# Fused linear attention and top-8 MLP on one Trainium2 core: the fifth spread copy moved ahead of a q unit, one product of M put into other PSUM banks, and M's copies put ahead of the q phis

## The chip, the cores and the metric

The kernel runs on one core of one Trainium2 chip. The metric is the device time of one execution in microseconds (us), as the median of the runs shown. Work is spread over the core's engines, each with its own queue of instructions in program order: TensorE (PE; its weight loads are listed apart as PEld), VectorE (DVE), ScalarE (ACT), GpSimd (POOL) and SyncE (SP, which here only issues transfers). They wait for each other through semaphores.

## The reference

The input x has 2048 tokens of width 640. The result is x plus two branches.

```
xn = layernorm(x)
q, k, v = split(xn @ wqkv)                    # 32 heads of 20
phi(t) = where(t > 0, t + 1, exp(t)) + 1e-6
kv = phi(k)^T v ; z = sum over tokens of phi(k)          # per head
o = (phi(q) kv) / (phi(q) z + 1e-6) @ wo

r = x @ w_r ; idx = the 8 tokens with the largest r
y = ((silu(x[idx] @ w_gate) * (x[idx] @ w_up)) @ w_down) * sigmoid(r[idx])
out = x + o + (x with y added at the rows idx)
```

## The kernel before

**Tiles and names.** Tokens stand in 16 tiles of 128, the width 640 in five blocks of 128. `ps` is the whole of PSUM: 8 banks of 512 f32 per partition, given out by number. `xnT` is the normalised input, transposed; `pqT` is phi(q), transposed (five blocks `m` by 2048 tokens). A "q unit" `u` is one block by 512 tokens: five matmuls into one bank (`q_mm`, L244), two ACT operations (`q_act`, L256 and L257: exp and relu) and one DVE operation that joins them into `pqT` (`q_phi`, L263). Units 0 to 12 are made in the main loop; this case is about units 13 to 19.

**Attention as one matrix.** The sum over tokens is made once (`GT`), turned into masked `kvT`, and joined with `wo` into a matrix M of five blocks (`M_sb`, in the tile named `late`). Block `m` of M is four matmuls into two banks (`m_mm`, L627) and one DVE copy out of them (`m_copy`, L636). The output of a token tile is then `pqT` times M (`o_mm`, L757), ten matmuls of 320 columns, plus the residual row (`o_add`, L767), and a store (L774).

**The denominators.** For each half of the tokens (`h`, 1024 tokens), `den_mm` and `den_act` make the inverse denominators `rd`. For each block, `spread_mm` (L570) spreads them over 128 rows: four matmuls into one half of the four banks 0 to 3. A "spread copy" on ACT (L587) moves these 1024 columns into one of the two halves of `spw`, and a DVE multiplication (L591) scales the block of `pqT` with them. Half 0 needs five such copies and scalings before the first output tile; half 1 is done within the output phase (L788 and L794).

**The MLP.** For the 8 chosen tokens, `hm` and its transpose `hT` are made, then come the down products (L712, 48 small matmuls into bank 4), their scaling on DVE into `y_sb` (L719), and an indirect DMA from POOL that adds the eight rows into a DRAM copy of x plus xn (`xxd`, L722). After it SP reloads the residual rows from `xxd` (L729), in pieces of 1, 1, 2, 2 and 2 tiles, then two pieces of four.

**Order.** The kernel is written out by hand (`manual_schedule`): on each engine the instructions stand in the order of the Python text, and the waits between engines follow from which instruction reads or overwrites what. Between the down products and the outputs the text goes on with M's blocks 1 to 4 in banks 6 and 7, q units 14 to 16 in banks 5, 4 and 5, and the fifth spread of half 0; then units 17 to 19 in banks 0, 1 and 2.

Of the kernel before, what the change touches and what calls it, by code (L numbers as in the profile page):

```python
# [9 lines left out]
S = 2048  # L10
# [10 lines left out]
HALF = S // 2  # L21
# [13 lines left out]
ALU = mybir.AluOpType  # L35
# [8 lines left out]
def kernel(  # L44
# [13 lines left out]
    nc = tc.nc  # L58
# [14 lines left out]
    def sb(shape, dt, name, pool=None, tag=None):  # L73
        return (pool or big).tile(shape, dt, tag=tag or name, name=name)
# [4 lines left out]
    pqT = sb([P, KC, S], BF16, "pqT")  # L79
# [29 lines left out]
    ps = psum.tile([P, 8, 512], F32, tag="ps", name="ps")  # L109
# [131 lines left out]
    def q_mm(u, b, lo=0, hi=KC):  # L241
        m, tb = QU[u]
        for kc in range(lo, hi):
            nc.tensor.matmul(  # L244
                ps[:, b, :],
                lhsT=wq_sb[:, kc, m * P : (m + 1) * P],
                rhs=xnT[:, kc, tb * TBLK : (tb + 1) * TBLK],
                start=(kc == 0), stop=(kc == KC - 1),
            )
# [3 lines left out]
    def q_act(u, b):  # L253
        e = evq.tile([P, TBLK], BF16, tag="eq", name=f"eq{u}")
        r = evq.tile([P, TBLK], BF16, tag="rq", name=f"rq{u}")
        nc.scalar.activation(e[:], ps[:, b, :], AF.Exp)  # L256
        nc.scalar.activation(r[:], ps[:, b, :], AF.Relu)  # L257
        qbuf[u] = (e, r)

    def q_phi(u):  # L260
        m, tb = QU[u]
        e, r = qbuf.pop(u)
        nc.vector.scalar_tensor_tensor(  # L263
            out=pqT[:, m, tb * TBLK : (tb + 1) * TBLK], in0=e[:], scalar=1.0, in1=r[:],
            op0=ALU.min, op1=ALU.add,
        )
# [11 lines left out]
    def grest_mm(t, c0, c1, b):  # L278
        for c in range(c0, c1):
            nc.tensor.matmul(  # L280
                ps[:, b, (c - c0) * P : (c - c0 + 1) * P],
                lhsT=xn[:, t, c * P : (c + 1) * P],
                rhs=pk[:, t, 512:D],
                start=(t == 0 and c == c0), stop=(t == T - 1),
                skip_group_check=True,
            )
# [198 lines left out]
    for t in range(T - 1):  # L485
# [3 lines left out]
        out=candm[:], in0=cand[:].unsqueeze(2).to_broadcast([T, 2, T, C]),  # L489
        in1=diag[:].unsqueeze(1).unsqueeze(3).to_broadcast([T, 2, T, C]), op=ALU.mult,  # L490
# [16 lines left out]
    for t in range(9):  # L507
# [11 lines left out]
        out=allc[:], in0=ps[:, 5, P : 2 * P], in1=tileoff[:].rearrange("p t c -> p (t c)"),  # L519
        op=ALU.add,  # L520
# [4 lines left out]
        out=junk[:, 0:C], in0=posu[:], scalar=1.0, in1=oh8[:], op0=ALU.mult, op1=ALU.mult,  # L525
# [3 lines left out]
        out=junk[:], in0=iot[:], scalar=pcol[:, 0:1], in1=allc[:], op0=ALU.is_equal,  # L529
# [4 lines left out]
        out=idxw[:, 1:2], in0=pcol[:, 1:2], scalar1=yoff[:, 0:1], scalar2=yoff[:, 1:2],  # L534
        op0=ALU.mult, op1=ALU.add,
    )
    for i in range(C):
# [5 lines left out]
        out=zm[:], in0=zT[:].rearrange("p (k h) -> p k h", k=KC), in1=headg[:], op=ALU.mult  # L543
# [24 lines left out]
    def spread_mm(h, m, half_bank):  # L568
        for j in range(4):
            nc.tensor.matmul(  # L570
                ps[:, j, 256 * half_bank : 256 * half_bank + 256],
                lhsT=grep[32 * j : 32 * j + 32, m * P : (m + 1) * P],
                rhs=rdens[h][32 * j : 32 * j + 32, :],
                start=True, stop=True, skip_group_check=True,
                tile_position=(32 * j, 0),
            )

    spw = big.tile([P, 2, 4, 256], BF16, tag="wk_sb", name="spw")
    nsp = [0]

    def spread_mul(h, m, half_bank, via_act, then=None, args=()):
        src = ps[:, 0:4, 256 * half_bank : 256 * half_bank + 256]
        dst = pqT[:, m, h * HALF : (h + 1) * HALF].rearrange("p (j f) -> p j f", j=4)
        if via_act:
            w = spw[:, nsp[0] % 2, :, :]
            nsp[0] += 1
            nc.scalar.copy(w, src)  # L587
            src = w
        if then is not None:
            then(*args)  # L590
        nc.vector.tensor_tensor(out=dst, in0=dst, in1=src, op=ALU.mult)  # L591

    den_mm(0, 6)
    den_act(0, 6)
# [29 lines left out]
    def m_mm(m, b):  # L624
        for h in range(2):
            for j in range(2):
                nc.tensor.matmul(  # L627
                    ps[DB * j : DB * j + DB, b + h, 0:HW],
                    lhsT=kvT[:, 2 * m + j, :],
                    rhs=wo_sb[:, 2 * m + j, h * HW : (h + 1) * HW],  # L630
                    start=True, stop=True,
                    tile_position=(0, DB * j),
                )

    def m_copy(m, b):
        nc.vector.tensor_copy(  # L636
            M_sb[:, m, :].rearrange("p (b f) -> p b f", b=2), ps[:, b : b + 2, 0:HW]
        )


    def gu_mm(w, b):
        for kc in range(KC):
            for j in range(4):
                nc.tensor.matmul(
                    ps[32 * j : 32 * j + 32, b, 0:FJ],
                    lhsT=xsT[:, kc, :],
                    rhs=w[:, kc, j * FJ : (j + 1) * FJ],
                    start=(kc == 0), stop=(kc == KC - 1),
                    tile_position=(0, 32 * j),
                )  # L650
# [10 lines left out]
    def q_unit(u, b):  # L661
        q_mm(u, b)
        q_act(u, b)

    nc.vector.scalar_tensor_tensor(
        out=junk[:, 0:C], in0=gv[:], scalar=1.0, in1=oh8[:], op0=ALU.mult, op1=ALU.mult,
# [10 lines left out]
    spread_mm(0, 1, 1)  # L677
    for t in range(9, T):
        grest_mm(t, 0, 4, 7)
    spread_mul(0, 0, 0, True)  # L680
    nc.vector.tensor_copy(
        GT[:, 0:4, 512:D], ps[:, 7, :].rearrange("p (c f) -> p c f", c=4)
    )
    for t in range(T):
        grest_mm(t, 4, 5, 6)
    nc.vector.tensor_copy(GT[:, 4, 512:D], ps[:, 6, 0:P])
    spread_mul(0, 1, 1, True)
    gu_mm(wg_sb, 5)
    nc.scalar.activation(e1, ps[:, 5, 0:FJ], AF.Exp, scale=-1.0)
    kv_mm(8, 10, 6, 8)  # L690
# [12 lines left out]
    q_mm(13, 5, 3)  # L703
    nc.vector.tensor_copy(hT, psb(4)[:, 0:FJ].rearrange("p (b c) -> p b c", b=3))
    m_copy(0, 6)
    spread_mul(0, 2, 0, True)
    spread_mul(0, 3, 1, True)
    q_act(13, 5)
    for fc in range(FC):
        j, b = fc // 3, fc % 3  # L710
# [9 lines left out]
        out=y_sb[:], in0=ps[:, 4, 0:YW], scalar1=gcol[:, 3:4], scalar2=None, op0=ALU.mult  # L720
# [2 lines left out]
        xxd[:], bass.IndirectOffsetOnAxis(ap=idxw[:, 1:2], axis=0), y_sb[:], None,  # L723
        compute_op=ALU.add,
    )
    q_phi(13)

    def reload(t0, t1):
        nc.sync.dma_start(x_sb[:, t0:t1, :], xxd_v[:, t0:t1, :])  # L729
# [2 lines left out]
        reload(t0, t1)  # L732
    m_mm(1, 6)
    m_copy(1, 6)
    spread_mm(0, 4, 0)
    q_unit(14, 5)
    spread_mul(0, 4, 0, True)
    m_mm(2, 6)
    m_copy(2, 6)
    q_phi(14)  # L740
    q_unit(15, 4)
    m_mm(3, 6)
# [2 lines left out]
    q_unit(16, 5)  # L745
    m_mm(4, 6)
    m_copy(4, 6)
    q_phi(16)
    for u in range(17, 20):
        q_unit(u, u - 17)  # L750
# [29 lines left out]
    scaled = []  # L780

    def spread_1(*ms):
        for i, m in enumerate(ms):
            spread_mm(1, m, i)
        for i, m in enumerate(ms):
            w = spw[:, nsp[0] % 2, :, :]
            nsp[0] += 1
            nc.scalar.copy(w, ps[:, 0:4, 256 * i : 256 * i + 256])  # L788
            scaled.append((m, w))

    def scale_1():
        m, w = scaled.pop(0)
        dst = pqT[:, m, HALF:S].rearrange("p (j f) -> p j f", j=4)
        nc.vector.tensor_tensor(out=dst, in0=dst, in1=w, op=ALU.mult)  # L794

    MID = {1: den_1, 2: lambda: spread_1(0, 1), 4: lambda: spread_1(2, 3)}
    END = {2: lambda: reload(8, 12), 4: lambda: reload(12, 16), 5: lambda: spread_1(4)}
    for t in range(T):
        b = (4, 6)[t % 2] if t < 8 else (0, 2, 4, 6)[t % 4]
        if t < T - 1:  # L800
            cols, banks = ((0, HW), (HW, D)), (b, b + 1)
            o_mm(t, cols, banks, 0, 2)
            if t in MID:
                MID[t]()
            o_mm(t, cols, banks, 2)
            o_add(t, b, 0, D)
            o_store(nc.sync if t % 2 == 0 else nc.scalar, t, 0, D)
        else:
            for i, (c0, c1, bb) in enumerate(((0, HW, b), (HW, 512, b + 1), (512, D, 0))):
                o_mm(t, ((c0, c1),), (bb,))  # L810
                o_add(t, bb, c0, c1)
                o_store(nc.scalar if i == 1 else nc.sync, t, c0, c1)
        if t in END:
            END[t]()
        if 2 <= t <= 5:
            scale_1()
        if t == 5:
            scale_1()
# [30 lines left out]
```

## Time and profile before

| What | us |
|---|---|
| median of 3 runs | 117.46 (117.32 to 117.6) |
| the profiled execution | 117.55 |
| its span, first to last instruction | 115.8 |
| PE busy in the span | 107.8 |
| DVE busy | 87.1 |
| ACT busy | 62.1 |
| POOL busy | 33.0 |

The profile is of one execution. It says for each engine how long it was busy, what each idle stretch waited for, and which chain of work ended last. In a row of the timeline the first number is the start in us from the beginning of the span, the second the time; `x4` says that four instructions are merged; in square brackets stands the idle time of the engine just before, and what ended it. `L627` is a line of the kernel.

### The profile page before, as it was taken

How to read it: one execution, taken by the hardware profiler on the slowest of the kernel's cores; microseconds unless marked ns; L12 is line 12 of the kernel's file. 1: busy time of each engine (PE TensorE's matmuls, PEld its weight loads, DVE VectorE, ACT ScalarE, POOL GpSimd, SP SyncE). 2: the span in 40 equal slices, each digit the busy share in tenths (PEclk: the TensorE clock that was granted, in tenths of full speed). 3: DMA queues.
4: the chain of work that ended last, by engine and by line, in shares of the span. 5: the costliest groups of instructions: out<-in, count | busy, mean ns of one | idle time of the engine just before them, and what ended most of it. 6: DMA issues, size and time to landing. Idle time of an engine off the chain costs nothing.

```text
span 115.8 us, 2502 instructions
## 1 busy us (share of the span) xinstructions
PE 107.8 (93%) x922; PEld 62.7 (54%) x922; DVE 87.1 (75%) x182; ACT 62.1 (54%) x123; POOL 33.0 (28%) x85
## 2 busy tenths in 40 slices
PE   5999996999999999999999999997699999999990
PEld 2445453555555555555555688543235666677770
DVE  0867999599997999877898927488695568695571
ACT  1568734755578555687555936593739465500000
POOL 7305357838777664500000023004100000000000
PEclk9999999999999999999999999999999999999999
DMA  3999379806999999999565994000286026985333
GB/s 108 307 378 332 64 175 180 216 0 140 273 229 235 265 369 146 312 365 339 184 226 182 262 382 147 6 0 0 14 230 228 24 89 156 301 282 178 113 113 113
DMA packets 23814, 22.20 MB, mean 192 GB/s; under 512 B 10074, under 2 KB 22522, under 8 KB 23802
## 3 DMA queue, kind: packets, MB, share of 16 engines
q1 hardware_dynamic: 21824, 19.99, 61.2%
q10 hardware_dynamic: 1834, 2.02, 5.1%
q0 software_dynamic: 144, 0.04, 0.5%
q8 instruction: 7, 0.11, 0.4%
q14 instruction: 5, 0.04, 0.1%
HBM read 14.62 MB, written 5.28 MB: 172 GB/s over the span
## 4 chain that ended last, share of the span: by engine, by line
PE 66%; DVE 13%; issue 6%; ACT 5%; DMA 4%; POOLq 3%; POOL 1%; ACTq 0%; DVEq 0%
PE ps L244 17%; PE ps L210 14%; PE ps L757 14%; PE ps L271 11%; DMA xnT<-xn 4%; PE ps L291 3%; POOLq L538 3%; DVE st L165 1%; DVE xn L767 1%; DVE xn L180 1%; DVE pk L233 1%; PE ps L627 1%; ACT spw L788 1%; DVE st L162 1%; PE ps L192 1%
## 5 line engine op out<-in xcount | busy, mean ns | idle before, releaser
L210 PE MATMUL ps<-wk_sb,xnT 128*128 128x320 bf16 (+1 forms) x160 | 25.2, 301 | 1.2 <-DMA xnT<-xn 1.0
L244 PE MATMUL ps<-xnT,wq_sb 128*128 128x512 bf16 x100 | 24.7, 379 | 0.1
L757 PE MATMUL ps<-late,pqT 128*128 128x320 bf16 (+2 forms) x165 | 22.6, 295 | 0.0
L226 ACT ACTIVATE ek<-ps 128x640 bf16<-128x640 f32 x16 | 11.3, 704 | 18.9 <-PE ps L210 18.9
L210 PEld LDWEIGHTS <-xnT 128*128 128x128 bf16 x160 | 15.3, 98 | 10.7 <-DMA xnT<-xn 1.7
L271 PE MATMUL ps<-pk,xn 128*128 128x512 bf16 x80 | 20.1, 379 | 0.2 <-DVE pk L233 0.2
L757 PEld LDWEIGHTS <-pqT 128*128 128x128 bf16 x165 | 15.6, 98 | 6.6 <-issue 0.6
L767 DVE TENSOR_TENSOR xn<-ps,x_sb 128x640 bf16<-128x640 f32 (+3 forms) x18 | 13.1, 748 | 5.6 <-PE ps L757 5.6
L263 DVE SCALAR_TENSOR_TENSOR pqT<-eq,rq 128x512 bf16<-128x512 bf16 x20 | 14.3, 714 | 3.8 <-ACT rq L257 3.8
L233 DVE SCALAR_TENSOR_TENSOR pk<-ek,rk 128x640 bf16<-128x640 bf16 x16 | 13.4, 838 | 3.5 <-ACT rk L227 3.3
L256 ACT ACTIVATE eq<-ps 128x512 bf16<-128x512 f32 x20 | 12.3, 617 | 4.4 <-PE ps L244 4.4
L244 PEld LDWEIGHTS <-wq_sb 128*128 128x128 bf16 x100 | 9.3, 97 | 9.7 <-issue 1.0
L271 PEld LDWEIGHTS <-xn 128*128 128x128 bf16 x80 | 7.7, 98 | 9.4 <-issue 0.5
L257 ACT ACTIVATE rq<-ps 128x512 bf16<-128x512 f32 x20 | 12.3, 616 | 0.0
L171 POOL TENSOR_TENSOR rs<-rs,half 128x1 f32<-128x1 f32 x14 | 11.1, 794 | 1.1
L227 ACT ACTIVATE rk<-ps 128x640 bf16<-128x640 f32 x16 | 11.2, 697 | 0.0
L162 DVE BATCH_NORM_STATS2 st<-x_sb 128x6 f32<-128x320 bf16 x16 | 7.7, 484 | 3.3 <-DMA x_sb<-in_A_x_dram 3.2
L168 POOL TENSOR_TENSOR rs<-mv,half 128x1 f32<-128x1 f32 x14 | 5.3, 377 | 15.6 <-DVE mv L166 15.4
L180 DVE TENSOR_SCALAR xn<-x_sb,mv,rs 128x640 bf16<-128x640 bf16 x16 | 7.7, 484 | 0.9 <-ACT rs L176 0.7
L539 POOL COPY xsT<-xnT 128x5 bf16 x8 | 1.7, 207 | 22.3 <-DMA xxd<-x_sb 18.9
L165 DVE BATCH_NORM_STATS2 st<-x_sb 128x6 f32<-128x320 bf16 x16 | 7.6, 476 | 0.0
L186 DVE TENSOR_TENSOR x_sb<-x_sb,xn 128x640 bf16<-128x640 bf16 x16 | 6.9, 475 | 0.0
(118 smaller groups left out, 103.1 us busy)
## 6 DMA issues: line engine op xcount, KB each, us to landing
x_sb<-in_A_x_dram SPq DMA_DIRECT2D x6, 320.0 KB, 4.3
wg_sb<-in_B_w_gate_dram SPq DMA_DIRECT2D x5, 384.0 KB, 5.2
wu_sb<-in_B_w_up_dram SPq DMA_DIRECT2D x5, 384.0 KB, 4.1
wd_sb<-in_B_w_down_dram SPq DMA_DIRECT2D x3, 640.0 KB, 8.5
xxd<-x_sb SPq DMA_DIRECT2D x2, 640.0 KB, 3.2
out_dram<-xn SPq DMA_DIRECT2D x8, 160.0 KB, 1.9
x_sb<-xxd SPq DMA_DIRECT2D x2, 640.0 KB, 5.4
out_dram<-xn ACTq DMA_DIRECT2D x7, 160.0 KB, 1.8
```

Source lines behind the costliest of these rows:

```text
L171: nc.gpsimd.tensor_tensor(out=rs[:, 1:2], in0=rs[:, 0:1], in1=half[:, 1:2], op=ALU.pow)
L210: nc.tensor.matmul(ps[:, b + h, 0:w], lhsT=xnT[:, kc, t * P : (t + 1) * P], rhs=wk_sb[:, kc, h * HW : h * HW + w], start=(kc == 0), stop=( ...
L226: nc.scalar.activation(e[:], ps[:, b : b + 2, 0:HW], AF.Exp)
L227: nc.scalar.activation(r[:], ps[:, b : b + 2, 0:HW], AF.Relu)
L233: nc.vector.scalar_tensor_tensor(out=pk[:, t, :].rearrange("p (b f) -> p b f", b=2), in0=e[:], scalar=1.0, in1=r[:], op0=ALU.min, op1=ALU.add,
L244: nc.tensor.matmul(ps[:, b, :], lhsT=wq_sb[:, kc, m * P : (m + 1) * P], rhs=xnT[:, kc, tb * TBLK : (tb + 1) * TBLK], start=(kc == 0), stop ...
L256: nc.scalar.activation(e[:], ps[:, b, :], AF.Exp)
L257: nc.scalar.activation(r[:], ps[:, b, :], AF.Relu)
L263: nc.vector.scalar_tensor_tensor(out=pqT[:, m, tb * TBLK : (tb + 1) * TBLK], in0=e[:], scalar=1.0, in1=r[:], op0=ALU.min, op1=ALU.add,)
L271: nc.tensor.matmul(ps[:, c, :], lhsT=xn[:, t, c * P : (c + 1) * P], rhs=pk[:, t, 0:512], start=(t == 0), stop=(t == T - 1),)
L757: nc.tensor.matmul(ps[:, b, 0 : c1 - c0], lhsT=pqT[:, kc, t * P : (t + 1) * P], rhs=M_sb[:, kc, c0:c1], start=(kc == 0), stop=(kc == KC - 1),)
L767: nc.vector.tensor_tensor(out=xn[:, t, c0:c1].rearrange("p (b f) -> p b f", f=w), in0=ps[:, b : b + n, 0:w], in1=x_sb[:, t, c0:c1].rearran ...
```

## The change

Three things change in the part between the down products and the outputs. The fifth spread copy of half 0 stands on ACT ahead of unit 14's two operations, no longer behind them. Block 2 of M goes to banks 0 and 1, which the fifth spread copy has read, no longer to 6 and 7. On DVE, `m_copy(1)` goes ahead of the scaling of block 3 and of unit 13's phi, and the scaling of block 4 goes behind `m_copy(4)`. To say this, the helper that copied and scaled is split into `spread_copy` and `scale_by`; the output phase uses the two, with the same instructions as before.

```diff
-    def spread_mul(h, m, half_bank, via_act, then=None, args=()):
-        src = ps[:, 0:4, 256 * half_bank : 256 * half_bank + 256]
+    def spread_copy(h, m, half_bank):
+        w = spw[:, nsp[0] % 2, :, :]
+        nsp[0] += 1
+        nc.scalar.copy(w, ps[:, 0:4, 256 * half_bank : 256 * half_bank + 256])
+        return w
+
+    def scale_by(h, m, w):
         dst = pqT[:, m, h * HALF : (h + 1) * HALF].rearrange("p (j f) -> p j f", j=4)
...
-        nc.vector.tensor_tensor(out=dst, in0=dst, in1=src, op=ALU.mult)
+        nc.vector.tensor_tensor(out=dst, in0=dst, in1=w, op=ALU.mult)
+
+    def spread_mul(h, m, half_bank):
+        scale_by(h, m, spread_copy(h, m, half_bank))
...
     m_copy(0, 6)
-    spread_mul(0, 2, 0, True)
-    spread_mul(0, 3, 1, True)
+    spread_mul(0, 2, 0)
+    w3 = spread_copy(0, 3, 1)
     q_act(13, 5)
...
-    q_phi(13)
...
     m_mm(1, 6)
     m_copy(1, 6)
+    scale_by(0, 3, w3)
+    q_phi(13)
     spread_mm(0, 4, 0)
+    w4 = spread_copy(0, 4, 0)
     q_unit(14, 5)
-    spread_mul(0, 4, 0, True)
-    m_mm(2, 6)
-    m_copy(2, 6)
+    m_mm(2, 0)
+    m_copy(2, 0)
     q_phi(14)
     q_unit(15, 4)
     m_mm(3, 6)
...
     m_mm(4, 6)
     m_copy(4, 6)
+    scale_by(0, 4, w4)
     q_phi(16)
```

What stands on the engines. Line numbers of the changed kernel differ a little: L589 is the scaling (L591 before), L637 the copy of M (L636 before), L720 the scaling into `y_sb` (L719 before), L584 the spread copy (L587 before), L628 the product of M (L627 before). `eq` and `rq` are a unit's two ACT results; the numbers in these names are only names.

DVE from `m_copy(0)` to unit 16's phi, before:

```order
L636 CAST late<-ps 128x640
L591 TENSOR_TENSOR pqT<-pqT,spw 128x1024 x2
L719 TENSOR_SCALAR y_sb<-ps,gcol 128x160
L263 SCALAR_TENSOR_TENSOR pqT<-eq_1308,rq_1309 128x512
L636 CAST late<-ps 128x640
L591 TENSOR_TENSOR pqT<-pqT,spw 128x1024
L636 CAST late<-ps 128x640
L263 SCALAR_TENSOR_TENSOR pqT<-eq_1382,rq_1383 128x512
L636 CAST late<-ps 128x640
L263 SCALAR_TENSOR_TENSOR pqT<-eq_1399,rq_1400 128x512
L636 CAST late<-ps 128x640
L263 SCALAR_TENSOR_TENSOR pqT<-eq_1414,rq_1415 128x512
```

and now:

```order
L637 CAST late<-ps 128x640
L589 TENSOR_TENSOR pqT<-pqT,spw 128x1024
L720 TENSOR_SCALAR y_sb<-ps,gcol 128x160
L637 CAST late<-ps 128x640
L589 TENSOR_TENSOR pqT<-pqT,spw 128x1024
L263 SCALAR_TENSOR_TENSOR pqT<-eq_1307,rq_1308 128x512
L637 CAST late<-ps 128x640
L263 SCALAR_TENSOR_TENSOR pqT<-eq_1383,rq_1384 128x512
L637 CAST late<-ps 128x640
L263 SCALAR_TENSOR_TENSOR pqT<-eq_1398,rq_1399 128x512
L637 CAST late<-ps 128x640
L589 TENSOR_TENSOR pqT<-pqT,spw 128x1024
```

The scaling of block 3 has moved from ahead of `y_sb` to behind `m_copy(1)`, unit 13's phi has moved behind both, and the scaling of block 4 from between `m_copy(1)` and `m_copy(2)` to behind `m_copy(4)`. The number of operations is the same.

ACT from the spread copies of blocks 2 and 3 to unit 15, before:

```order
L587 CAST spw<-ps 128x1024 x2
L256 ACTIVATE eq_1308<-ps 128x512
L257 ACTIVATE rq_1309<-ps 128x512
L256 ACTIVATE eq_1382<-ps 128x512
L257 ACTIVATE rq_1383<-ps 128x512
L587 CAST spw<-ps 128x1024
L256 ACTIVATE eq_1399<-ps 128x512
L257 ACTIVATE rq_1400<-ps 128x512
```

and now:

```order
L584 CAST spw<-ps 128x1024 x2
L256 ACTIVATE eq_1307<-ps 128x512
L257 ACTIVATE rq_1308<-ps 128x512
L584 CAST spw<-ps 128x1024
L256 ACTIVATE eq_1383<-ps 128x512
L257 ACTIVATE rq_1384<-ps 128x512
L256 ACTIVATE eq_1398<-ps 128x512
L257 ACTIVATE rq_1399<-ps 128x512
```

The fifth spread copy has moved past unit 14's two operations.

PE at the end of unit 14 and the start of block 2 of M, before, with what each instruction waits for:

```order
L244 LDWEIGHTS wq_sb
L244 MATMUL ps<-xnT,wq_sb 128x512
L627 LDWEIGHTS kvT
L627 MATMUL ps<-wo_sb,kvT 64x320 [waits DVE_49]
L627 LDWEIGHTS kvT
```

and now:

```order
L244 LDWEIGHTS wq_sb
L244 MATMUL ps<-xnT,wq_sb 128x512
L628 LDWEIGHTS kvT
L628 MATMUL ps<-wo_sb,kvT 64x320 [waits Activation_49]
L628 LDWEIGHTS kvT
```

PE's order is the same; block 2's first matmul waits for ACT (the fifth spread copy), where it waited for DVE (`m_copy(1)`).

More of the change, by code (lines that the diff above doesn't have):

```diff
@@ L579 @@
     nsp = [0]
-    def spread_mul(h, m, half_bank, via_act, then=None, args=()):
-        src = ps[:, 0:4, 256 * half_bank : 256 * half_bank + 256]
-        dst = pqT[:, m, h * HALF : (h + 1) * HALF].rearrange("p (j f) -> p j f", j=4)
[L584 to L591, printed above, removed]
+    def spread_copy(h, m, half_bank):
[4 more added lines that the diff above has]
+    def scale_by(h, m, w):
+        dst = pqT[:, m, h * HALF : (h + 1) * HALF].rearrange("p (j f) -> p j f", j=4)
+        nc.vector.tensor_tensor(out=dst, in0=dst, in1=w, op=ALU.mult)
+    def spread_mul(h, m, half_bank):
+        scale_by(h, m, spread_copy(h, m, half_bank))
     den_mm(0, 6)
@@ L679 @@
         grest_mm(t, 0, 4, 7)
-    spread_mul(0, 0, 0, True)
+    spread_mul(0, 0, 0)
     nc.vector.tensor_copy(
@@ L686 @@
     nc.vector.tensor_copy(GT[:, 4, 512:D], ps[:, 6, 0:P])
-    spread_mul(0, 1, 1, True)
+    spread_mul(0, 1, 1)
     gu_mm(wg_sb, 5)
@@ L785, in spread_1 @@
         for i, m in enumerate(ms):
[L786 to L789, printed above, removed]
+            scaled.append((m, spread_copy(1, m, i)))
     def scale_1():
-        m, w = scaled.pop(0)
-        dst = pqT[:, m, HALF:S].rearrange("p (j f) -> p j f", j=4)
-        nc.vector.tensor_tensor(out=dst, in0=dst, in1=w, op=ALU.mult)
+        scale_by(1, *scaled.pop(0))
     MID = {1: den_1, 2: lambda: spread_1(0, 1), 4: lambda: spread_1(2, 3)}
```

## The prediction

> **What bounds the kernel now.** I read the page first, then what TensorE waited for from 70 us to the end, then the timeline of each engine around these waits.
>
> ```profile
> span 115.8 us, 2502 instructions
> PE 107.8 (93%) x922; PEld 62.7 (54%) x922; DVE 87.1 (75%) x182; ACT 62.1 (54%) x123; POOL 33.0 (28%) x85
> PE ps L627 <- DVE late L636: 1.9, 2, 1.1
> PE ps L570 <- ACT spw L788: 0.2, 1, 0.2
> ```
>
> TensorE is busy for 93% of the span, so only its idle time can be won without taking work away. From 70 us on it waited twice for M's copies, 1.9 us in all, and once for 0.2 us. Both long waits lie in the part that the change rewrites:
>
> ```profile
> 78.20 0.46 PE L627 MATMUL ps<-wo_sb,kvT 80*64 80x320 bf16 x4
> 78.59 0.29 PE L570 MATMUL ps<-rd,grep 32*128 32x256 bf16 x4
> 78.81 1.25 PE L244 MATMUL ps<-xnT,wq_sb 128*128 128x512 bf16 x5
> 79.94 0.82 DVE L636 CAST late<-ps 128x640 bf16<-128x640 f32 x1
> 80.00 0.11 PEld L627 LDWEIGHTS <-kvT 80*64 80x64 bf16 x1 [0.42 <-issue]
> 80.81 0.46 PE L627 MATMUL ps<-wo_sb,kvT 80*64 80x320 bf16 x4 [0.74 <-DVE late L636]
> 81.08 1.02 ACT L587 CAST spw<-ps 128x1024 bf16<-128x1024 f32 x1
> 81.20 1.25 PE L244 MATMUL ps<-xnT,wq_sb 128*128 128x512 bf16 x5
> 82.13 0.69 DVE L591 TENSOR_TENSOR pqT<-pqT,spw 128x1024 bf16<-128x1024 bf16 x1 [1.37 <-ACT spw L587]
> 82.39 0.11 PEld L627 LDWEIGHTS <-kvT 80*64 80x64 bf16 x1 [0.42 <-issue]
> 82.74 0.82 DVE L636 CAST late<-ps 128x640 bf16<-128x640 f32 x1
> 83.61 0.46 PE L627 MATMUL ps<-wo_sb,kvT 80*64 80x320 bf16 x4 [1.15 <-DVE late L636]
> 84.00 1.25 PE L244 MATMUL ps<-xnT,wq_sb 128*128 128x512 bf16 x5
> 85.18 0.14 PEld L627 LDWEIGHTS <-kvT 80*64 80x64 bf16 x4 [0.42 <-issue]
> 85.58 3.41 PE L244 MATMUL ps<-xnT,wq_sb 128*128 128x512 bf16 x15
> 88.83 2.06 PE L757 MATMUL ps<-late,pqT 128*128 128x320 bf16 x14
> ```
>
> Block 2 of M writes banks 6 and 7 and so waits for `m_copy(1)`, which ends at 80.76; its matmul starts at 80.81. Block 3 waits for `m_copy(2)`, which ends at 83.56. That one is late for another reason: it stands on DVE behind the scaling of block 4, and DVE stood idle 1.37 us until ACT had made the fifth spread copy (81.08 to 82.10), itself behind unit 14's two ACT operations. From 85.58 TensorE runs without such a wait.
>
> **The change part by part.** Nothing is added or removed: PE, DVE and ACT each have the same operations in another order. So the sum is the two waits, less what the new order makes TensorE wait for.
>
> *What the waits are worth.* Without a wait, a block's first matmul starts with its weight load (four loads at 85.18). The loads that were ready stand at 80.00 and 82.39; the matmuls came at 80.81 and 83.61. That gives 0.81 + 1.22 = 2.03 us. (The page's 0.74 and 1.15 are smaller because they count from a modelled end of the matmul in front.)
>
> *Block 2 in banks 0 and 1.* It now waits for the fifth spread copy. That copy needs its four spread matmuls (end 78.59 + 0.29 = 78.88), a free ACT, and the half of `spw` that the scaling of block 2 has read.
>
> ```profile
> 77.77 0.59 ACT L257 ACTIVATE rq<-ps 128x512 bf16<-128x512 f32 x1
> 77.85 1.28 DVE L591 TENSOR_TENSOR pqT<-pqT,spw 128x1024 bf16<-128x1024 bf16 x2
> 79.05 0.38 DVE L719 TENSOR_SCALAR y_sb<-ps,gcol 128x160 bf16<-128x160 f32 x1
> 79.34 0.68 DVE L263 SCALAR_TENSOR_TENSOR pqT<-eq,rq 128x512 bf16<-128x512 bf16 x1
> 80.10 0.60 ACT L256 ACTIVATE eq<-ps 128x512 bf16<-128x512 f32 x1 [1.75 <-PE ps L244]
> 80.60 0.59 ACT L257 ACTIVATE rq<-ps 128x512 bf16<-128x512 f32 x1
> ```
>
> ACT is free at 78.36 and idles until 80.10, which is the cover: the copy's 1.02 us fit into those 1.75. The first of the two scalings ends at 77.85 + 0.69 = 78.54. So the copy starts at 78.88 + 0.04 (the step from unit 14's end at 80.06 to its exp at 80.10) = 78.92 and ends at 79.94. With 0.05 to the next engine (80.76 to 80.81) block 2 may start at 79.99; TensorE comes there at 80.00. This is even, so the price is between 0 and 0.1; I take 0.03. Unit 14's exp is not held up, since ACT is free again before 80.06. If the copy ran late, block 2, unit 15 and all behind them would wait by as much.
>
> *DVE's new order.* From the rows above, starts follow each other by 0.60 after a scaling or a phi, 0.29 after `y_sb` and 0.73 after a copy of M. Scaling 2 starts at 77.85, `y_sb` 78.44, `m_copy(1)` 78.73 (its matmuls end at 78.66), scaling 3 79.46, unit 13's phi 80.06, `m_copy(2)` 80.66 (block 2 ends at 80.46), unit 14's phi 81.40 (its relu ends at 81.19). On TensorE unit 15 follows at 80.39 and block 3 at 81.58, for which `m_copy(1)` was done at 79.55; so that wait is gone. Block 3 ends at 82.04, `m_copy(3)` starts at 82.09 and ends at 82.91. Block 4 is due at 83.16 and may start at 82.96: a margin of 0.20, the thinnest of the new order beside the even one. Unit 17 writes bank 0, which `m_copy(2)` leaves at 81.48, two us before it.
>
> *What moved later.* Unit 13's phi ends at 80.74; the exp of unit 15, which reuses its buffer, is due at 81.69. The scaling of block 4 now starts behind `m_copy(4)` at about 84.40 and ends at 85.09; the first output needs it after 88.83 - 2.03 = 86.80. Unit 16's phi ends at 85.68; the exp of unit 18, which waits for it, is due at 85.92. These cost nothing with margins of 0.95, 1.7 and 0.24.
>
> *What the tail does with it.*
>
> ```profile
> 83.32 2.31 SPq L729 DMA_DIRECT2D x_sb<-xxd  x5
> x_sb<-xxd SPq DMA_DIRECT2D x2, 160.0 KB, 2.1
> 90.14 0.69 DVE L263 SCALAR_TENSOR_TENSOR pqT<-eq,rq 128x512 bf16<-128x512 bf16 x1 [0.39 <-ACT rq L257]
> 90.75 0.82 DVE L767 TENSOR_TENSOR xn<-ps,x_sb 128x640 bf16<-128x640 f32 x1
> 91.48 1.53 PE L757 MATMUL ps<-late,pqT 128*128 128x320 bf16 x10
> 99.25 12.35 PE ps L757 x90
> ```
>
> The last row is of the chain of waits: the end hangs on TensorE's output products. All else in the output phase hangs on TensorE, ACT and DVE work that moves along. Only the residual rows don't: they hang on `y_sb`, which is 0.61 earlier (78.44 for 79.05), not 2.03. Tile 0's rows now land at 83.32 + 2.1 = 85.4, so at 84.8 then; the first output addition will want them at 90.75 - 2.03 = 88.72. That leaves 3.9 us.
>
> *Sum.* 2.03 - 0.03 = 2.00 us. The profiled execution took 117.55 with a span of 115.8; it becomes 115.55 with 113.8. It lies 0.09 above the median of the runs, so the median becomes 117.46 - 2.00 = 115.46, **rounded 115.5**.
>
> **The rivals.**
>
> *POOL and DVE get in each other's way.* [...] Now POOL works from about 79.12 to 81.05, and scaling 3 and unit 13's phi, each with two inputs from SBUF, start inside that time. The trace has a place where such operations met POOL's, beside the same ones apart:
>
> ```profile
> 79.73 1.93 POOL L722 DMA_INDIRECT xxd<-y_sb,idxw  x1 [7.27 <-DVE y_sb L719]
> 22.98 1.19 POOL L141 TENSOR_SCALAR_AFFINE_SELECT grep<-grep 32x640 bf16<-32x640 bf16 x1
> 28.36 0.72 POOL L141 TENSOR_SCALAR_AFFINE_SELECT grep<-grep 32x640 bf16<-32x640 bf16 x1
> 22.43 1.16 DVE L233 SCALAR_TENSOR_TENSOR pk<-ek,rk 128x640 bf16<-128x640 bf16 x1 [1.22 <-ACT rk L227]
> 26.03 0.77 DVE L233 SCALAR_TENSOR_TENSOR pk<-ek,rk 128x640 bf16<-128x640 bf16 x1
> 23.52 1.20 DVE L263 SCALAR_TENSOR_TENSOR pqT<-eq,rq 128x512 bf16<-128x512 bf16 x1
> 27.02 0.69 DVE L263 SCALAR_TENSOR_TENSOR pqT<-eq,rq 128x512 bf16<-128x512 bf16 x1 [0.22 <-ACT rq L257]
> ```
>
> They lost 0.39 and 0.51 there. By these rows `m_copy(3)` comes 0.90 later, block 4 starts 0.90 - 0.25 = 0.65 late (0.20 of margin and 0.05 by which DVE waits for block 3 anyway), and the time is 116.1. At worst scaling 3 stands until POOL is done at 81.05, 1.59 late: block 4 is 1.34 late, 116.8. [...]
>
> *Thin margins.* If every DVE step takes 0.08 more than assumed, the eight steps ahead of block 4 use up 0.25 and cost 0.4 more; with a spread copy late by 0.1 that is 115.9 to 116.0. For it speaks only that the margins are 0.01 and 0.20.
>
> *The copy isn't early.* If the fifth spread copy had to wait for the scaling of block 3 (the other half of `spw`, done at 80.15), it would end at 81.2, block 2 start at 81.25 and block 3 at 82.83 for 83.61: 0.78 won, 116.7. Against it: the two halves are apart in the tile.
>
> *Slower: the residual rows come too late.* DVE has no gap from 77.85 to 82 now, while before it idled 1.37 us during POOL's work; if DVE holds POOL off, the indirect DMA is late. The price: bank 4, which the third output tile needs at about 92.3 - 2.03 = 90.27 (of the ten products from 91.48 on, the first six still belong to the second tile), is freed 0.87 after tile 0 has landed (the addition's 0.82 and 0.05), so landing beyond 89.4 costs one for one, and beyond 91.4 the kernel is slower than before. That needs a slip of 6.6 us. POOL held off until DVE's first gap near 83.5 would slip 4.4 and land at 89.2, which costs nothing; so only a much longer hold loses.
>
> **How the numbers follow.** Forecast 0.68; POOL and DVE 0.17 (116.1 to 116.8); thin margins 0.06; copy not early 0.03; residual rows late 0.06, half of that about even and half slower. About 0.2% (0.23 us) is what a measurement here tells from no change. Faster takes all but the last: 0.94; same 0.03; slower 0.03. The likeliest case's own range is 115.2 to 115.8, from the spread of the runs (0.14 to each side) and the price of the copy up to 0.1 and a little of the margins. For 8 in 10 the range takes in thin margins and the milder half of the contention: 115.2 to 116.4.
>
> **What would show it.** Right: TensorE's waits for M's copies gone from the list; block 2 starting at 80.0 to 80.1 behind the spread copy, which runs from 78.9; block 3 near 81.6, block 4 near 83.2; the output products starting near 86.8, and the chain ending on them as before. POOL and DVE: scaling 3 or unit 13's phi longer than 0.69 or starting late, and a wait ahead of block 4. Late rows: the first addition waiting for a transfer. The forecast is wrong if TensorE shows over 0.3 us of new waits before the output products, or if these grow in the tail.

## The result

The changed kernel is faster: 116.15 us (median of 4 runs, 115.56 to 116.9) for 117.51 (4 runs, 117.32 to 117.6). The ratio on record is 0.9858, with a 95% interval of 0.9809 to 0.9906; it isn't the quotient of the two medians, which is 0.9884 and lies inside the interval (the ratios below likewise). The forecast was 115.5, with 115.2 to 116.4. Medians, ranges and ratios, here and below, leave out runs more than 1.5% above the fastest of their kernel, so that fewer are counted than were made; the profiled run of "DVE's order only" (118.57 us) is one of those.

The page of the profile of the changed kernel and its list of what TensorE waited for from 70 us on (us in all, times, longest):

```profile
span 115.1 us, 2496 instructions
PE 108.6 (94%) x914; PEld 63.3 (55%) x922; DVE 86.9 (75%) x182; ACT 62.3 (54%) x123; POOL 32.9 (29%) x85
PE ps L570 <- ACT spw L584: 0.2, 1, 0.2
```

The two waits for M's copies, 1.9 us before, are gone; the one of 0.2 us in the output phase is left as it was. The timeline of the part that was rewritten, all engines:

```profile
78.59 1.01 PE L713 MATMUL ps<-wd_sb,late 128*32 128x160 bf16 x48
79.78 0.38 DVE L720 TENSOR_SCALAR y_sb<-ps,gcol 128x160 bf16<-128x160 f32 x1
80.08 0.82 DVE L637 CAST late<-ps 128x640 bf16<-128x640 f32 x1
80.15 1.25 PE L244 MATMUL ps<-xnT,wq_sb 128*128 128x512 bf16 x4
80.27 1.01 ACT L584 CAST spw<-ps 128x1024 bf16<-128x1024 f32 x1 [0.58 <-PE ps L570]
80.47 1.77 POOL L723 DMA_INDIRECT xxd<-y_sb,idxw  x1 [6.67 <-DVE y_sb L720]
80.81 0.68 DVE L589 TENSOR_TENSOR pqT<-pqT,spw 128x1024 bf16<-128x1024 bf16 x1
81.33 0.46 PE L628 MATMUL ps<-wo_sb,kvT 80*64 80x320 bf16 x4
81.41 0.69 DVE L263 SCALAR_TENSOR_TENSOR pqT<-eq,rq 128x512 bf16<-128x512 bf16 x1
82.01 0.82 DVE L637 CAST late<-ps 128x640 bf16<-128x640 f32 x1
82.91 0.46 PE L628 MATMUL ps<-wo_sb,kvT 80*64 80x320 bf16 x4
83.42 0.82 DVE L637 CAST late<-ps 128x640 bf16<-128x640 f32 x1
83.90 2.31 SPq L729 DMA_DIRECT2D x_sb<-xxd  x5
84.49 0.46 PE L628 MATMUL ps<-wo_sb,kvT 80*64 80x320 bf16 x4
88.13 2.06 PE L760 MATMUL ps<-late,pqT 128*128 128x320 bf16 x14
90.06 0.82 DVE L770 TENSOR_TENSOR xn<-ps,x_sb 128x640 bf16<-128x640 f32 x1
```

Blocks 2, 3 and 4 of M start at 81.33, 82.91 and 84.49, in the pace of TensorE alone and with nothing in brackets. (Some matmul records are missing, so `x4` stands where a unit has five.) The chain of waits still ends on the output products: 90 of them, 12.35 us from 98.55 on.

But the first down product, which no part of the change can reach, comes at 78.59 for 77.25 before. So the profiled execution, 116.9 us, is made of two parts:

| us | before | after | difference |
|---|---|---|---|
| start to the first down product | 77.25 | 78.59 | +1.34 |
| first down product to the end of the span | 38.55 | 36.51 | -2.04 |

Where the first part differs is seen in the first microseconds. The timeline of TensorE before:

```profile
6.56 0.69 PE L210 MATMUL ps<-wk_sb,xnT 128*128 128x320 bf16 x3
8.13 1.68 PE L210 MATMUL ps<-wk_sb,xnT 128*128 128x321 bf16 x11
10.19 2.31 PE L210 MATMUL ps<-wk_sb,xnT 128*128 128x320 bf16 x14
```

and after:

```profile
6.68 0.98 PE L210 MATMUL ps<-wk_sb,xnT 128*128 128x320 bf16 x3
8.78 2.53 PE L210 MATMUL ps<-wk_sb,xnT 128*128 128x321 bf16 x11
11.43 2.31 PE L210 MATMUL ps<-wk_sb,xnT 128*128 128x320 bf16 x14
```

The same first products of K, the same lines, take about half as long again: 0.98 for 0.69, 2.53 for 1.68. The next fourteen take 2.31 in both and start 1.24 later (11.43 for 10.19), which is nearly all of the 1.34. By the groups by shape, one product of 320 columns takes 464 ns between 6.5 and 7.5 us after, and 300 ns between 12 and 77 us. The late start belongs to this execution and not to the change: a second execution of the changed kernel, below, has its first down product at 77.51. The time from the first down product to the end, called *the part behind* below, is therefore the measure of what an edit does, beside the times. It is right to about 0.05 us, since the span is shown with one decimal. The time from the first down product to the first output product (L757 before, L760 after) has no such rounding: 88.83 - 77.25 = 11.58 us before, 88.13 - 78.59 = 9.54 after, again 2.04 less.

### The profile page after: what moved, and what is told of

Read it like the earlier page. It is cut to its first block, busy times and chain, and to the rows that moved or that the text cites. A ratio compares the mean times of both kernels' runs of the same rounds, so it can differ in the third digit from the quotient of the medians.

```text
span 115.1 us, 2496 instructions
## 1 busy us (share of the span) xinstructions
PE 108.6 (94%) x914; PEld 63.3 (55%) x922; DVE 86.9 (75%) x182; ACT 62.3 (54%) x123; POOL 32.9 (29%) x85
## 4 chain that ended last, share of the span: by engine, by line
PE 68%; DVE 11%; DMA 6%; issue 5%; POOLq 3%; ACT 3%; ACTq 0%; DVEq 0%; POOL 0%
PE ps L244 18%; PE ps L210 18%; PE ps L760 14%; PE ps L271 11%; DMA xnT<-xn 4%; POOLq L538 3%; DMA x_sb<-in_A_x_dram 2%; DVE xn L770 1%; PE ps L628 1%; PE ps L192 1%; DVE pk L233 1%; DVE st L162 1%; DVE st L165 1%; ACT spw L584 1%; DVE xn L180 1%
## 5 line engine op out<-in xcount | busy, mean ns | idle before, releaser
L210 PE MATMUL ps<-wk_sb,xnT 128*128 128x320 bf16 (+1 forms) x160 | 26.6, 312 | 1.1 <-DMA xnT<-xn 1.1
L760 PE MATMUL ps<-late,pqT 128*128 128x320 bf16 (+2 forms) x165 | 22.6, 295 | 0.0
L760 PEld LDWEIGHTS <-pqT 128*128 128x128 bf16 x165 | 15.6, 98 | 6.6 <-issue 0.6
L584 ACT CAST spw<-ps 128x1024 bf16<-128x1024 f32 x10 | 9.7, 1014 | 5.4 <-PE ps L570 4.2
L162 DVE BATCH_NORM_STATS2 st<-x_sb 128x6 f32<-128x320 bf16 x16 | 7.7, 481 | 3.5 <-DMA x_sb<-in_A_x_dram 3.5
L589 DVE TENSOR_TENSOR pqT<-pqT,spw 128x1024 bf16<-128x1024 bf16 x10 | 6.8, 684 | 1.5 <-ACT spw L584 1.5
```

The costliest lines, as they stand in the source:

```text
L210: nc.tensor.matmul(ps[:, b + h, 0:w], lhsT=xnT[:, kc, t * P : (t + 1) * P], rhs=wk_sb[:, kc, h * HW : h * HW + w], start=(kc == 0), stop=( ...
L760: nc.tensor.matmul(ps[:, b, 0 : c1 - c0], lhsT=pqT[:, kc, t * P : (t + 1) * P], rhs=M_sb[:, kc, c0:c1], start=(kc == 0), stop=(kc == KC - 1),)
```

## The experiments

Theory: the gain of 2.0 us is the two waits, each removed by making early what TensorE waited for, and it holds whatever the start does. Rivals: the late start belongs to the change; all three parts are needed; the banks alone do it; the tail gives the gain back when the residual rows are late. Of 10 profiled executions of the kernels of this study:

| kernel | first down product, us | from it to the first output product | part behind, us | median of its runs, us (kernel before beside it) | runs counted, of those made | ratio, 95% interval |
|---|---|---|---|---|---|---|
| before | 77.25 | 11.58 | 38.55 | 117.51 | 4 of 4 | |
| changed | 78.59 | 9.54 | 36.51 | 116.15 (117.51) | 4 of 4 | 0.9809 to 0.9906 |
| changed, once more | 77.51 | 9.54 | 36.59 | 115.77 (117.77) | 5 of 6 | 0.9781 to 0.9890 |
| DVE's order only | 80.29 | 9.54 | 36.51 | 115.73 (117.77) | 5 of 7 | 0.9763 to 0.9847 |
| fifth copy only | 77.23 | 10.36 | 37.37 | 116.50 (117.77) | 6 of 6 | 0.9839 to 0.9918 |
| banks only | 77.53 | 11.69 | 38.67 | 117.70 (117.77) | 6 of 12 | 0.9948 to 1.0012 |
| fifth copy and banks | 77.48 | 9.87 | 36.92 | 116.08 (117.75) | 6 of 6 | 0.9775 to 0.9887 |
| residual rows late | 77.29 | 9.54 | 38.81 | 118.10 (117.75) | 7 of 10 | 0.9994 to 1.0106 |
| last spread later | 78.80 | 9.54 | 36.30 | 115.63 (117.75) | 5 of 6 | 0.9741 to 0.9886 |
| warm-up with ones | 77.45 | 9.54 | 36.55 | 115.76 (117.75) | 5 of 6 | 0.9746 to 0.9885 |

The kernel before was run 17 times beside each of two groups of experiments (117.77 and 117.75 in the table), and 15 are counted in each.

### The changed kernel once more

No edit.

> The changed kernel once more. Theory: the change is worth 2.0 us behind the first down product, whatever lies ahead of it: 36.5 us from the first down product to the end of the span (38.55 before), and the first 77 to 79 us differ from execution to execution by how long the first K products run slow (about 455 ns for one of 320 columns where 300 is usual). So times between 115.5 and 116.9, and the kernel before, run as often on the same chip, shows a spread of its own of up to 1 us. Rival: the late start belongs to the changed kernel; then the kernel before stays within 0.3 us over all its runs while this one spreads.

Measured: 115.77 us median (115.54 to 116.86, 5 runs) for 117.77 of the kernel before (15 runs); ratio 0.9835 (0.9781 to 0.989). The part behind is 36.59; to the first output product it is 9.54 as in the first execution, so the 0.08 between the two is rounding of the span. The kernel before, in its 15 runs on this chip, ranged from 117.5 to 118.73, where the four runs of the result had lain within 0.28. So the rival falls: both kernels spread. That the spread of the kernel before lies in its start as well isn't shown, as only one of its executions has a profile here. The difference of the two medians is 2.00 us.

### DVE's order only

```diff
     spread_mm(0, 4, 0)
-    w4 = spread_copy(0, 4, 0)
     q_unit(14, 5)
-    m_mm(2, 0)
-    m_copy(2, 0)
+    w4 = spread_copy(0, 4, 0)
+    m_mm(2, 6)
+    m_copy(2, 6)
```

(against the changed kernel)

> Only DVE's new order; the fifth spread copy stays behind unit 14's two ACT operations and block 2 of M stays in banks 6 and 7. Theory (a wait goes when what TensorE waits for comes early on DVE): m_copy(1) ends near 79.55 and m_copy(2) near 81.5 counted from the before's 77.25 for the first down product, so both blocks start without a wait, with a margin of only 0.05 for block 3; the scaling of block 4 stands behind m_copy(4) and no longer waits in front of anything. 36.5 to 36.7 us from the first down product to the end. Rival (all three parts are needed, the late spread copy costs its 1.22): 37.7 or more.

Measured: the part behind 36.51 us, the whole gain; the median, 115.73 us, is that of the changed kernel (115.77) but for 0.04; ratio 0.9805 (0.9763 to 0.9847). Timeline of this kernel, TensorE, DVE and ACT:

```profile
83.03 0.46 PE L628 MATMUL ps<-wo_sb,kvT 80*64 80x320 bf16 x4
83.71 0.81 DVE L637 CAST late<-ps 128x640 bf16<-128x640 f32 x1
84.11 1.02 ACT L584 CAST spw<-ps 128x1024 bf16<-128x1024 f32 x1
84.61 0.46 PE L628 MATMUL ps<-wo_sb,kvT 80*64 80x320 bf16 x4
```

The fifth spread copy ends at 85.13, after block 3 has started, and nothing waits for it: its scaling stands behind `m_copy(4)`. Block 3, in banks 6 and 7 again, starts without a wait 0.09 after `m_copy(2)` has ended (84.52). So with DVE's new order the other two parts together add nothing here (9.54 us to the first output product with and without them). The rival that all three are needed falls. DVE's order with just one of the two wasn't run, nor were its own two moves (`m_copy(1)` ahead, the scaling of block 4 behind) run apart.

### The fifth copy only, and the banks only

The fifth copy only, against the kernel before (the helper is split as in the change):

```diff
     spread_mm(0, 4, 0)
+    w4 = spread_copy(0, 4, 0)
     q_unit(14, 5)
-    spread_mul(0, 4, 0, True)
+    scale_by(0, 4, w4)
     m_mm(2, 6)
```

> Only the fifth spread copy ahead of unit 14's two ACT operations; DVE's order and the banks as before. Theory: block 2 still waits for m_copy(1) (0.81), DVE no longer idles for the copy, m_copy(2) ends near 82.15 and block 3 starts without a wait: 1.22 won, 37.3 us from the first down product to the end. Rival (the two waits have one cause, DVE being full): 38.0 or more.

Measured: the part behind 37.37 us; ratio 0.9878 (0.9839 to 0.9918). Its timeline:

```profile
80.79 0.46 PE L628 MATMUL ps<-wo_sb,kvT 80*64 80x320 bf16 x4 [0.74 <-DVE late L637]
81.29 0.82 DVE L637 CAST late<-ps 128x640 bf16<-128x640 f32 x1
82.36 0.46 PE L628 MATMUL ps<-wo_sb,kvT 80*64 80x320 bf16 x4
```

Block 2 waits as before, block 3 no longer: `m_copy(2)` ends at 82.11, where before it ended at 83.56. The part behind is 1.18 us shorter, and the first output product comes 11.58 - 10.36 = 1.22 earlier, as expected. The two waits do have two causes.

The banks only, against the kernel before:

```diff
-    m_mm(2, 6)
-    m_copy(2, 6)
+    m_mm(2, 0)
+    m_copy(2, 0)
```

> Only block 2 of M in banks 0 and 1; ACT's and DVE's order as before. Theory: block 2 now waits for the fifth spread copy in its old place (82.10 by the clock of the profile before) and starts 1.3 us later than before, block 3 then finds m_copy(1) long done and starts at about 83.7 for 83.6: nothing won or lost, 38.5 to 38.8 us from the first down product to the end. Rival (the banks are what frees TensorE): 0.8 won, 37.7.

Measured: the part behind 38.67 us; ratio 0.998 (0.9948 to 1.0012).

```profile
82.42 0.46 PE L627 MATMUL ps<-wo_sb,kvT 80*64 80x320 bf16 x4 [2.08 <-ACT spw L587]
83.99 0.46 PE L627 MATMUL ps<-wo_sb,kvT 80*64 80x320 bf16 x4
```

One wait of 2.08 us in place of the two of 0.74 and 1.15, and 0.11 lost to the first output product. The banks alone only exchange the wait for DVE by one for ACT: block 2 starts when the late spread copy is done. What the changed kernel would have paid with a late copy wasn't run; this is the nearest to it.

### The fifth copy and the banks, without DVE's order

```diff
     spread_mm(0, 4, 0)
+    w4 = spread_copy(0, 4, 0)
     q_unit(14, 5)
-    spread_mul(0, 4, 0, True)
-    m_mm(2, 6)
-    m_copy(2, 6)
+    scale_by(0, 4, w4)
+    m_mm(2, 0)
+    m_copy(2, 0)
```

> The fifth spread copy ahead of unit 14's two ACT operations and block 2 of M in banks 0 and 1, DVE's order as before (m_copy(1) behind the scaling of block 3 and unit 13's phi, the scaling of block 4 ahead of m_copy(2)). Theory: blocks 2 and 3 start without a wait, but DVE's chain is then 0.5 longer ahead of m_copy(3), which ends near 83.45 counted from 77.25 for the first down product, so block 4 waits about 0.35: 36.9 us from the first down product to the end (36.5 in the changed kernel, 38.55 before). Rival (only DVE's order helps): 37.7 or more.

Measured: the part behind 36.92 us; ratio 0.9831 (0.9775 to 0.9887).

```profile
82.83 0.82 DVE L637 CAST late<-ps 128x640 bf16<-128x640 f32 x1
83.70 0.46 PE L628 MATMUL ps<-wo_sb,kvT 80*64 80x320 bf16 x4 [0.26 <-DVE late L637]
```

Blocks 2 and 3 are free, block 4 waits 0.26 us (0.35 expected) for `m_copy(3)`, which ends at 83.65; counted to the first output product, 0.33 us is lost (9.87 for 9.54). So there are two ways to the first 1.7 us (11.58 - 9.87): let the copies of M run early on DVE, or take block 2 out of banks 6 and 7 and bring the spread copy forward. The last 0.33 us came only with DVE's order.

### The residual rows late

In the changed kernel, the scaling into `y_sb`, the indirect DMA and the first five reloads stand behind the scaling of block 4, and unit 15 goes to bank 3:

```diff
-    (scaling into y_sb, indirect DMA, reloads of tiles 0 to 7)
     m_mm(1, 6)
...
-    q_unit(15, 4)
+    q_unit(15, 3)
...
     scale_by(0, 4, w4)
+    (scaling into y_sb, indirect DMA, reloads of tiles 0 to 7)
     q_phi(16)
```

> The changed kernel with the scaling into y_sb, the indirect DMA and the first five reloads put behind the scaling of block 4 on DVE, that is 6.6 us later; unit 15 goes to bank 3, since bank 4 is then read late. Theory: tile 0's residual rows land 6.6 later, the first output addition waits for them, and beyond 4.7 us of slip TensorE pays one for one, because the third output tile needs bank 4 back: 1.9 lost, 38.4 us from the first down product to the end. Rival (the reloads are hidden anyway): 36.5 to 36.8; rival (the slack was smaller, 3.9 or less): 39 or more.

Measured: the part behind 38.81 us, 2.3 more than the changed kernel.

```profile
85.03 0.38 DVE L741 TENSOR_SCALAR y_sb<-ps,gcol 128x160 bf16<-128x160 f32 x1
85.72 1.93 POOL L744 DMA_INDIRECT xxd<-y_sb,idxw  x1 [13.23 <-DVE y_sb L741]
89.39 2.32 SPq L721 DMA_DIRECT2D x_sb<-xxd  x5
91.74 1.55 DVE L770 TENSOR_TENSOR xn<-ps,x_sb 128x640 bf16<-128x640 f32 x2 [2.84 <-DMA x_sb<-xxd]
92.61 0.70 PE L760 MATMUL ps<-late,pqT 128*128 128x320 bf16 x4 [2.14 <-DVE xn L770]
```

Counted from the first down product, `y_sb` starts 7.74 here and 1.19 in the changed kernel: 6.55 later. The first addition now waits for its rows, and the third output tile for bank 4: 2.14 us by the brackets, which count from a modelled end. By the starts it is 2.29: the second tile's last six products start at 89.49, 0.14 apart, so the third tile was due at about 90.32 and came at 92.61. That is the 2.3 us lost. So the tail's slack is real and finite: 6.55 - 2.29 = 4.3 us, 0.4 less than the 4.7 expected, and the 38.81 lies between the theory's 38.4 and the 39 of the rival with the smaller slack. The way from the indirect DMA's start to the first reload was 3.67 us here (85.72 to 89.39) and 3.43 in the changed kernel (80.47 to 83.90), which is 0.24 of the 0.4; 0.16 of it is POOL's own operation (1.93 for 1.77).

### The last spread later

The one wait that was left (0.2 us, the fifth spread of half 1), against the changed kernel:

```diff
-    MID = {1: den_1, 2: lambda: spread_1(0, 1), 4: lambda: spread_1(2, 3)}
-    END = {2: lambda: reload(8, 12), 4: lambda: reload(12, 16), 5: lambda: spread_1(4)}
+    MID = {1: den_1, 2: lambda: spread_1(0, 1), 4: lambda: spread_1(2, 3), 6: lambda: spread_1(4)}
+    END = {2: lambda: reload(8, 12), 4: lambda: reload(12, 16)}
...
-        if t == 5:
+        if t == 6:
             scale_1()
```

> The changed kernel with the fifth spread of half 1 four matmuls later (inside the seventh output tile, no longer ahead of it) and its scaling behind the seventh addition. Theory: the one wait left behind the down products (0.2 us of TensorE for the copy ahead) goes, and the scaling is still done before the ninth tile's last block: 36.3 us from the first down product to the end. Rival: the scaling now comes too late and the ninth tile waits: 36.5 or more.

Measured: the part behind 36.30 us; the list of TensorE's waits no longer names the spread, whose row has nothing in brackets:

```profile
98.77 0.29 PE L570 MATMUL ps<-rd,grep 32*128 32x256 bf16 x4
```

The times, 115.63 us median (115.32 to 116.87, 5 runs), ratio 0.9813 (0.9741 to 0.9886), can't tell these 0.2 us from the changed kernel's; the start moves them more (78.59 and 77.51 to the first down product in two executions of the changed kernel). By the profile this version is 0.2 us ahead of the changed kernel; by the times that isn't shown.

### The warm-up with ones

The 9 matmuls that run on TensorE before there is data multiply a block of zeros; here it holds ones.

```diff
-    nc.gpsimd.memset(GT[:, 0, 0:512], 0.0)
+    nc.gpsimd.memset(GT[:, 0, 0:512], 1.0)
```

> The changed kernel with ones instead of zeros in the block that the warm-up matmuls multiply; nothing else differs. Theory (when TensorE reaches its full pace is chance, whatever the warm-up multiplies): the same spread of times as for the changed kernel, mostly 115.5 to 116.3 and some near 116.9, and 36.5 us from the first down product to the end. Rival (zeros count as little work, so that full pace comes late in some executions): all times within 0.3 us, at 115.5 or below.

Measured: 115.76 us median (115.3 to 116.61, 5 runs); ratio 0.9815 (0.9746 to 0.9885); the part behind 36.55. The spread stays, so the zeros aren't its cause.

## Why the prediction was right, and where it was off

**The two waits, 2.03 us: right.** The part behind became 2.04 shorter (1.96 in the second execution; to the first output product 2.04 in both). Reading a wait's worth from the weight load that was ready to the matmul that came, and not from the page's idle time, gave 2.03 where the page's two numbers give 1.89.

**The fifth spread copy, even, at 0.03: right.** It ran from 80.27 to 81.28; block 2 came at 81.33, as soon as unit 14 let it. The prediction's times, moved by 1.34, are 80.26, 81.28 and 81.34. The "banks only" run shows block 2 waiting for a late copy (2.08 us). The even hand-over is needed only because block 2 went to banks 0 and 1: with DVE's order alone, block 2 in banks 6 and 7, that copy ended two microseconds later and cost nothing.

**DVE's new order and the margin of 0.20: right.** `m_copy(3)` ended at 84.24 and block 4 started at 84.49: 0.25, of which 0.05 is the hand-over. DVE's eight starts from the scaling of block 2 (79.18) to `m_copy(3)` (83.42) came within 0.01 of the forecast ones moved by 1.34. What the prediction did not work out is that this order alone frees block 3 too, in banks 6 and 7: by its own times `m_copy(2)` is done at 81.48 and block 3 is due at 81.58. It costed the three parts together and left unsaid which carries the gain; the runs gave 36.51 us for DVE's order alone, as for all three.

**POOL and DVE in each other's way: fell.** The scaling of block 3 (0.68) and unit 13's phi (0.69) both ran inside POOL's 80.47 to 82.24, at their usual length, and POOL's 1.77 was shorter than before (1.93). In the profile before, too, the phi at 79.34 kept its 0.68, though POOL's operation began in it (79.73). The rows at 22 to 24 us, where such operations lost 0.39 and 0.51, were beside POOL's select on `grep` (L141, 1.19 from 22.98 on), not beside an indirect DMA; why DVE's operations took longer there and not here isn't shown. A scaling that stands until POOL is done, from which the rival's 116.8 is worked out, is shown by no run: scaling 3 started 0.34 after POOL did and was done at 81.49, 0.75 before it. POOL's own time did differ: 1.93 in the kernel before and with the residual rows late, where a unit's phi was running on DVE when it began, and 1.77 in the changed kernel, where a copy of M was; it was 1.77 also with DVE's order only and with the last spread later, where DVE's order is the same at this place. Why isn't shown.

**The copy isn't early: fell.** It started at 80.27, while the scaling of block 3 ran from 80.81 to 81.49. **Thin margins: fell**, the pace of TensorE was undisturbed. The prices of this rival and of the one before take 0.05 for the time that DVE waits for block 3 ahead of `m_copy(3)`; by the prediction's own starts (81.40 + 0.60 = 82.00, and 82.09) it is 0.09, which changes no case.

**The tail: right, and tested.** The first addition came at 90.06, without waiting for its rows. When `y_sb` was put 6.55 later, the chain that the rival names (rows, addition, bank 4, third tile) cost 2.29. If every slip beyond the slack costs as much, which one run can't show by itself, the slack is 4.3 us, where the rival's times (89.4 - 84.8) gave 4.6; the reloads came 0.24 later behind their DMA than in the changed kernel.

**The step that was off: the median.** The sum was made against a profiled execution that lay 0.09 from its median, and the start was taken as fixed, because three runs lay within 0.28. It wasn't: 1.34 us of the profiled execution after came ahead of the change. So 116.15 was measured for 115.5; with more runs of both, on one chip, 115.77 for 117.77, a difference of 2.00 where 2.00 was forecast. The term that was missing is the spread of the start: the changed kernel's own four runs lie 1.3 us apart, and in the one that has a profile the start is the reason. That 116.15 still fell inside the range is luck. It lies outside the 115.2 to 115.8 of the likeliest case, and the part above that was kept for thin margins and for POOL and DVE in each other's way, neither of which came.

## What to carry to other kernels

Here TensorE's waits were worth what lay between the ready weight load and the late matmul (2.03 us), and this moved to the end of the kernel undiminished (2.04), since every other input of the tail had slack, which can be worked out by row (about 4.3 us for the residual rows). Before parts are put together, work out each alone: here DVE's new order did the whole, and the banks and the early spread copy together nothing more. And where a kernel's start varies, measure an edit from a fixed instruction behind the start; here the median of four runs was 0.65 off the forecast, the part behind 0.04.

## What the runs showed of the hardware that was not expected

The first products on TensorE came at two paces, about 460 and 300 ns for one of 320 columns in the changed kernel's first execution, and when the pace changed varied between executions of one kernel. In seven of the ten profiled executions the eleven products near 8 to 10 us took about 1.68 us, and the first down product came at 77.2 to 77.5. In the changed kernel's first execution they took 2.53, and it came at 78.59; in "last spread later" 2.85, and it came at 78.80; with DVE's order only 3.15, with a wait of 0.69 for weights ahead of them, and it came at 80.29. The first two late starts look alike in the end but not in the records. The stretches to 12 us, in windows (length; busy time and instructions of PE, PEld, DVE, ACT and POOL; granted TensorE clock; DMA share; GB/s), in the changed kernel:

```profile
0.00:5.00 5.00, 3.63 (x10) 1.14 (x11) 1.45 (x4) 1.78 (x3) 3.26 (x13) 1.00 0.60 183
5.00:8.00 3.00, 2.89 (x17) 1.36 (x18) 2.08 (x6) 1.75 (x6) 0.00 (x0) 1.00 1.06 380
8.00:12.00 4.00, 4.00 (x27) 2.68 (x25) 2.28 (x7) 2.11 (x5) 1.70 (x4) 1.00 0.90 307
```

The clock shown is 1.00 in all three windows, though the products of the first 10 us are slow (453 to 475 ns on average for 320 or 321 columns from 6.5 to 10.5 us, 300 from 11 us on): here the granted clock does not show the slower pace. With the last spread later three products took 0.57 from 6.54 on, where they took 0.98 in the changed kernel's first execution, and the eleven from 8.59 on were slow again:

```profile
6.54 0.57 PE L210 MATMUL ps<-wk_sb,xnT 128*128 128x320 bf16 x3 [0.44 <-DMA wk_sb<-in_A_wqkv_dram]
7.57 0.69 PE L210 MATMUL ps<-wk_sb,xnT 128*128 128x320 bf16 x2 [0.35 <-DMA wk_sb<-in_A_wqkv_dram]
8.59 2.85 PE L210 MATMUL ps<-wk_sb,xnT 128*128 128x321 bf16 x11
```

and there the granted clock does show the slower pace, in windows:

```profile
7.50:8.00 0.50, 0.43 (x2) 0.25 (x2) 0.48 (x2) 0.18 (x1) 0.00 (x0) 0.59 1.02 358
8.00:8.50 0.50, 0.50 (x6) 0.44 (x5) 0.48 (x3) 0.00 (x0) 0.19 (x1) 0.50 1.10 356
...
11.00:11.50 0.50, 0.50 (x7) 0.42 (x6) 0.00 (x0) 0.50 (x2) 0.00 (x0) 1.00 0.80 269
```

It reads 0.59 from 7.5 to 8.0, so by an estimate 0.50 from about 7.6, if it fell there from 1.00 in one step, and 0.50 in every window up to 11.0: some 3.4 us at a granted clock of 0.50, behind two short waits for the first weights (0.44 and 0.35). In the changed kernel's first execution TensorE worked from about 1.4 us on with hardly a gap (3.63 of the first 5.00 us, 2.89 of the next 3.00), and the pace changed only between 10.5 and 11 us. What decides between an early and a late change isn't shown: a wait for the first weights of 0.66 us stood ahead of the products in the execution with ones too, which was not late, and in the changed kernel's first execution there was none.
